# Attention scores in four quarters of the array, a shorter expert part, other warming buffer, new order

## The chip, the cores and the metric

The kernel runs on one core of a Trainium2 chip. The metric is the time of one execution on the device in microseconds; the median of several runs counts. The core's engines work side by side and wait for each other through semaphores: TensorE (PE) multiplies matrices into PSUM, VectorE (DVE), ScalarE (ACT) and GpSimd (POOL) work element by element, SyncE (SP) issues most of the DMA transfers.

## The reference

Three layers follow each other: attention in a sliding window with a bias by distance, a dense layer with an activation between two products, and a layer of eight experts that only some tokens enter.

```python
scores = scale * np.matmul(q, k.transpose(0, 1, 3, 2))          # 4 batches, 8 heads, 576 positions, 64 wide
mask = (rel >= 0) & (rel < window)                              # window = 128
scores = np.where(mask, scores + bias[None], -1000000000.0)
attn = exp(scores - max) / (sum + 1e-09);  x = attn @ v         # 2304 tokens of 512
h = x @ w_in                                                    # 512 x 2048, float64 weights
g = np.where(pos, h, np.where(neg, 0.0, (h + beta) ** 2 / (4.0 * beta)))
x = g @ w_out                                                   # 2048 x 512
do_compute = x @ w_skip > 0                                     # tokens that an expert computes
```

Tokens with a score of zero or less keep their value. With the inputs used here all 2304 scores are negative (the largest is -0.06), so no expert is entered.

## The kernel before

The 2304 tokens are nine blocks `g` of 256 (two tiles of 128), the eight heads four pairs. Class `Fused` writes attention and the dense layer as pieces of work with costs, due times and buffers; a planner in the file (`Plan.order`, line 108) gives each piece an engine and a place by the constants `PLAN`, `ENGINES`, `LAT` and `SWITCH`, and `run` (line 592) emits the pieces in that order. So the order on each engine is fixed when the program is built, and a change of the constants changes it everywhere. `SWITCH` charges TensorE for going in and out of products that use a part of the array.

`pair(g, p)` (line 305) is the attention of one block for two heads. SP loads `qkraw` (L318) and `vraw` (L321). The queries are scaled on ACT or POOL (L328, L330). The scores (L340 and L343) put the two heads into the two row halves of the array: 128 queries as weights, 256 keys (the tile and the one ahead of it) streamed, in fp32, which the trace shows as two weight loads and two products for each. They fill both buffers of the PSUM ring `att`. DVE merges the two key tiles by a mask with a predicated copy (L354), adds the bias and takes the maximum (L359); ACT computes the exponentials and their sums (L365); DVE inverts the sums (L374, L375); ACT normalizes (L393); PE transposes (L401); ACT or DVE copies to `pts` (L286 and L288 are helper lines for copies); POOL cuts the result into its two triangles `ab` (L300); PE multiplies by the values (L423), the heads side by side in the column halves of the array; ACT and DVE split the result into the two parts of `xT`.

`tile_ff` (line 492) is one step of the dense layer on one block, 256 of the 2048 middle columns: 24 products into `h` (L504, each product in three parts of a split into high and low), the activation on ACT and DVE (L516, L521, L537), the split of `g` (L286, L295), and 12 products into `acc` (L546). Eight steps make a block. Blocks 0 and 1 alternate while the weights arrive; `weight` (line 440) turns float64 into a high and a low part on POOL (L453), DVE (L457, L461, L468) and ACT.

Two more things matter. `fill` (L590) is a product without use that keeps TensorE's clock up; `run` puts such products into gaps that the planner sees before 40 us, until two buffers of the ring `acc1` are taken; they write into one buffer of that ring, which the transposes of block 0 use too. And `moe2` (line 649) counts the selected tokens (L653 to L658); every engine reads the count (L659) and branches (L660) past the code of `route` and of eight copies of `expert` if it is zero. Before, `route` is written out for 18 tiles (8 records of transposes and 16 of products each on PE), and each copy of `expert` holds 304 weight loads and products for PE in its loop (16 for transposes, 8 x 36 for the rest).

Of the kernel before, what the change touches and what calls it, by code (L numbers as in the profile page):

```python
# [11 lines left out]
F32 = mybir.dt.float32  # L12
F32R = mybir.dt.float32r
# [8 lines left out]
P = 128  # L22
# [35 lines left out]
SWITCH = {"out": 0.09, "": 0.0, "rows": 0.2, "cols": 0.14}  # L58
# [37 lines left out]
class Plan:  # L96
# [47 lines left out]
    def forward(self, free, due):  # L144
# [32 lines left out]
        while len(log) < n:  # L177
# [28 lines left out]
            if e == "T" and p.mode != mode:  # L206
                free[e] = end = end + (SWITCH["out"] if mode else 0.0) + SWITCH[p.mode]
                mode = p.mode
# [35 lines left out]
class Fused:  # L244
# [60 lines left out]
    def pair(self, g, p, due):  # L305
# [3 lines left out]
        lo = 2 * t0 - 1 if g else 0  # L309
        n = 5 if g else 4  # L310
# [8 lines left out]
            out=qk.t[:, 0:n, :].rearrange("p t j -> p (t j)"),  # L319
            in_=a["qk"][hd, :, lo:lo + n, :].rearrange("h d t j -> (h d) (t j)")), n * P * P * 4, new=[qk])  # L320
# [4 lines left out]
        def scale(e):  # L325
            q = qk.t[:, j:n:2, :]
# [19 lines left out]
        sn = self.buf("sn", 2, [P, 4, P])  # L346
        sd = add({"T": 0.87 if g else 0.66}, scores, [lq], new=s + [sn], use=[qk], mode="rows")
        st = self.buf("st", 4, [P, 2, 4])
        exps = []
        for odd, o in heads:  # L350
            h = 2 * p + odd

            def merge(e, s=s[odd]):
                nc.vector.copy_predicated(s.t[:, 1 - j:2, 0, :], self.mask[:, 1 - j:2, :], s.t[:, 1 - j:2, 1, :])  # L354

            def rowmax(e, s=s[odd], odd=odd, h=h):
                for i in range(2):
                    x = 2 * odd + i
                    nc.vector.tensor_tensor_reduce(  # L359
                        out=sn.t[:, x, :], in0=s.t[:, i, 0, :], in1=self.nrel[:, TILE_TYPE.get(t0 + i, TYPE_N), :],  # L360
# [7 lines left out]
            d = add({"D": dve(128 * (1 + j))}, merge, [sd], use=[s[odd]])  # L368
# [477 lines left out]
```

## Time and profile before

| | us |
|---|---|
| median of three runs | 535.33 (535.31 to 537.53) |
| the profiled execution | 536.52 |
| its span, first to last instruction | 534.7 |
| mean granted TensorE clock | 0.988 |

| engine | busy us | share of the span |
|---|---|---|
| PE | 516.6 | 97% |
| DVE | 280.6 | 52% |
| ACT | 293.2 | 55% |
| POOL | 108.2 | 20% |

The busy time of PE counts pipelined products whose ends are modelled, so it is read together with the chain of work that ended last. A chain row gives the start and the time until the next link; a timeline row gives the start of the first and the end of the last of several like instructions. Line numbers are those of the kernel before.

### The profile page before, as it was taken

How to read it: one execution, taken by the hardware profiler on the slowest of the kernel's cores; microseconds unless marked ns; L12 is line 12 of the kernel's file. 1: busy time of each engine (PE TensorE's matmuls, PEld its weight loads, DVE VectorE, ACT ScalarE, POOL GpSimd, SP SyncE). 2: the span in 40 equal slices, each digit the busy share in tenths (PEclk: the TensorE clock that was granted, in tenths of full speed). 3: DMA queues.
4: the chain of work that ended last, by engine and by line, in shares of the span. 5: the costliest groups of instructions: out<-in, count | busy, mean ns of one | idle time of the engine just before them, and what ended most of it. 6: DMA issues, size and time to landing. Idle time of an engine off the chain costs nothing.

```text
span 534.7 us, 9520 instructions
## 1 busy us (share of the span) xinstructions
PE 516.6 (97%) x3460; PEld 434.0 (81%) x3460; DVE 280.6 (52%) x826; ACT 293.2 (55%) x782; POOL 108.2 (20%) x208
## 2 busy tenths in 40 slices
PE   7879999999999999999999999999999999999993
PEld 3466888888888789888888898878888888789882
DVE  6899998999435523453344423541455235523231
ACT  5887565586446733663456534763376347733330
POOL 2766352344100310022002200220013000210000
PEclk9799999999999999999999999999999999999997
DMA  7665554643211121112111210120112111001001
GB/s 262 190 206 165 190 180 132 207 148 111 70 41 49 52 59 40 50 50 60 41 40 35 85 40 25 51 69 17 39 51 80 31 40 50 5 26 40 1 0 47
DMA packets 27145, 41.14 MB, mean 77 GB/s; under 512 B 2001, under 2 KB 15953, under 8 KB 27089
## 3 DMA queue, kind: packets, MB, share of 16 engines
q1 hardware_dynamic: 26416, 40.12, 23.8%
q8 instruction: 29, 0.48, 0.4%
q10 hardware_dynamic: 672, 0.33, 0.2%
q14 instruction: 28, 0.22, 0.1%
HBM read 35.72 MB, written 4.72 MB: 76 GB/s over the span
## 4 chain that ended last, share of the span: by engine, by line
PE 90%; DVE 4%; DMA 2%; issue 1%; ACT 1%; POOL 1%; ACTq 0%; POOLq 0%
PE acc L546 38%; PE h L504 37%; PE att L343 6%; PE att L423 5%; PE att L401 2%; DMA stage<-in_w_in 1%; DMA vraw<-in_v 1%; DVE sn L359 1%; DVE wtmp L468 1%; DMA qkraw<-in_qk 1%; DVE stage L461 1%; DVE att L354 0%; DVE stage L457 0%; PE acc L401 0%; ACT sn L365 0%
## 5 line engine op out<-in xcount | busy, mean ns | idle before, releaser
L504 PE MATMUL h<-xT,wi 128*128 128x256 f32 x1728 | 221.4, 282 | 0.1
L546 PE MATMUL acc<-wo,g 128*128 128x512 f32 x864 | 220.6, 400 | 0.1
L504 PEld LDWEIGHTS h<-xT,wi 128*128 128x128 f32 x1728 | 212.5, 188 | 9.1 <-issue 4.4
L546 PEld LDWEIGHTS acc<-wo,g 128*128 128x128 f32 x864 | 155.5, 188 | 40.9 <-issue 6.2
L516 ACT ACTIVATE u<-h,half 128x512 f32<-128x512 f32 x72 | 49.3, 684 | 113.0 <-PE h L504 112.8
L537 DVE SCALAR_TENSOR_TENSOR h<-h,u 128x512 f32<-128x512 f32 x72 | 50.1, 696 | 111.7 <-ACT u L521 109.4
L300 POOL TENSOR_SCALAR_AFFINE_SELECT ab<-pts 128x256 f32<-128x256 f32 (+1 forms) x144 | 62.1, 463 | 96.4 <-DVE pts L288 68.1
L365 ACT ACTIVATE sn<-sn,st 128x128 f32<-128x128 f32 x144 | 56.1, 391 | 30.7 <-DVE st L359 30.7
L286 ACT ACTIVATE g<-h 128x512 fp32r<-128x512 f32 x72 | 42.7, 593 | 34.1 <-DVE h L537 34.0
L295 DVE TENSOR_TENSOR g<-h,g 128x512 fp32r<-128x512 f32 x72 | 49.5, 687 | 18.7 <-ACT g L286 17.5
L330 POOL TENSOR_SCALAR qkraw<-qkraw,qscale 128x256 f32<-128x256 f32 x21 | 11.4, 542 | 216.7 <-DMA qkraw<-in_qk 201.5
L393 ACT ACTIVATE sn<-sn,st 128x128 f32<-128x128 f32 x144 | 46.5, 390 | 0.5 <-DVE st L375 0.3
L521 ACT ACTIVATE u<-u 128x512 f32<-128x512 f32 x72 | 45.3, 629 | 1.8
L354 DVE COPY_PREDICATED att<-mask,att 128x256 f32<-128x256 uint8 (+1 forms) x72 | 26.5, 410 | 33.4 <-PE att L343 33.3
L343 PE MATMUL att<-qkraw 64*128 64x256 f32 x272 | 40.8, 413 | 1.3 <-DVE pts L288 1.3
L453 POOL TENSOR_SCALAR wtmp<-stage 128x512 f32<-128x512 f32 x32 | 26.5, 830 | 38.8 <-DVE wi L295 14.4
L359 DVE CUSTOM_DVE_ANT_0 sn<-att,nrel 128x128 f32<-128x128 f32 x144 | 33.3, 285 | 0.0
L343 PEld LDWEIGHTS att<-qkraw 64*128 64x128 f32 x272 | 24.6, 193 | 10.6 <-issue 5.1
L423 PE MATMUL att<-ab,vraw 128*64 128x128 f32 (+1 forms) x384 | 32.0, 313 | 1.2 <-DMA vraw<-in_v 0.6
L423 PEld LDWEIGHTS att<-ab,vraw 128*64 128x64 f32 x384 | 23.1, 137 | 9.3 <-issue 2.6
L561 DVE CUSTOM_DVE_ANT_0 junk<-acc,wskip 128x512 f32<-128x512 f32 x18 | 12.4, 691 | 32.9 <-ACT stage L286 32.3
L365 ACT ACTIVATION_READ_ACCUMULATOR sn<-sn,st 128x1 f32 x144 | 27.0, 188 | 0.0
(50 smaller groups left out, 280.8 us busy)
## 6 DMA issues: line engine op xcount, KB each, us to landing
qkraw<-in_qk SPq DMA_DIRECT2D x32, 320.0 KB, 3.0
stage<-in_w_in SPq DMA_DIRECT2D x16, 512.0 KB, 3.6
stage<-in_w_out SPq DMA_DIRECT2D x16, 512.0 KB, 3.7
vraw<-in_v SPq DMA_DIRECT2D x32, 192.0 KB, 2.7
out_x<-stage SPq DMA_DIRECT2D x18, 256.0 KB, 2.0
qkraw<-in_qk SPq DMA_DIRECT2D x4, 256.0 KB, 3.4
vraw<-in_v SPq DMA_DIRECT2D x4, 128.0 KB, 4.2
nrel<-in_nrel ACTq DMA_DIRECT2D x1, 256.0 KB, 3.8
```

The costliest lines, as they stand in the source:

```text
L286: self.nc.scalar.activation(out=out, in_=in_, func=AF.Copy)
L295: eng.tensor_tensor(out=out, in0=in0, in1=in1, op=ALU.subtract)
L300: self.nc.gpsimd.affine_select(out=out, in_=in_, pattern=[[0, n], [sign, P]], compare_op=ALU.is_ge if causal else ALU.is_gt, fill=0.0, base=0,
L343: nc.tensor.matmul(s[odd].t[:, i, :, :], qk.t[o, q, :], qk.t[o, q - 1:q + 2:2, :], start=True, stop=True)
L365: nc.scalar.activation(out=sn.t[:, x, :], in_=sn.t[:, x, :], func=AF.Exp, scale=-1.0, bias=st.t[:, 0, x:x + 1], accum_out=st.t[:, 1, x:x + 1])
L393: nc.scalar.activation(out=sn.t[:, x, :], in_=sn.t[:, x, :], func=AF.Copy, scale=st.t[:, 1, x:x + 1])
L423: nc.tensor.matmul(av.t[o, out, :], v.t[:, k, o], ab.t[:, m, :], start=not more, stop=True, skip_group_check=more)
L504: nc.tensor.matmul(h.t[:, c, :], w[:, wz, k, :], x.t[:, xz, k].rearrange("p a b -> p (a b)"), start=k == 0 and i == 0, stop=k == NKC - 1 a ...
L516: r = add({"A": 0.167 + 0.213 * n}, lambda e: nc.scalar.activation(out=uv(), in_=hv(), func=AF.Relu, scale=0.5, bias=self.half), [d], new= ...
L521: nc.scalar.activation(out=uv(), in_=uv(), func=AF.Square)
L537: r = add({"D": dve(256 * n)}, lambda e: nc.vector.scalar_tensor_tensor(out=hv(), in0=hv(), scalar=1.0, in1=uv(), op0=ALU.max, op1=ALU.min ...
L546: nc.tensor.matmul(acc[i].t, gt.t[:, gz, c, i * P:(i + 1) * P], self.wo[:, f, wz, :], start=f == 0 and j == 0, stop=f == NF - 1 and j == 2)
```

## The change

- The scores take 64 queries as weights and 192 keys as stream: those that the window of a half tile can touch. Each head's two halves write to the two partition halves of its PSUM bank, so the four products of a tile (two heads, two halves) each use one quarter of the array. `qk` is laid out anew in memory for this (three key tiles and two query tiles a block); the first tile of block 0 keeps its product of 128 by 128.
- The merge becomes two predicated copies, one for each half, over 64 partitions and 64 columns a tile.
- The expert part is one function with loops over blocks, experts and quarters of the middle width. On PE its loop bodies hold 48 records (routing a block of two tiles) and 72 (one quarter of the middle width).
- The warming products write to a buffer of the ring `h`, and they go on until two other `h` buffers are taken, that is until the second dense step.
- `PLAN`, `ENGINES`, `SWITCH` and some costs change, so all pieces get a new order; the rebias of weights (L453) goes from POOL to ACT, all scaling of queries to POOL, and the normalization may go to DVE.

```diff
-PLAN = dict(base=15.36, d0=9.433, d1=4.571, d2=5, lag=1, ahead=79.42, lead=5, spread=2.882, margin=1.102, slack=0.071,
-            fin=0.107, passes=5, first=0, stick=3.899, late=0, late_due=300)
-ENGINES = dict(norm="A", wlo="DP", rebias="P", pt="AD", whi="A", square="AP", scale="AP")
+PLAN = dict(base=10.991, d0=8.647, d1=6.176, d2=5.536, lag=1, ahead=65.777, lead=10.393, spread=5.669, margin=1.2,
+            slack=0.055, fin=0.23, passes=5, first=0, stick=6, late=0, late_due=120.077)
+ENGINES = dict(norm="AD", wlo="DP", rebias="A", pt="AD", whi="A", square="AP", scale="P")
-SWITCH = {"out": 0.09, "": 0.0, "rows": 0.2, "cols": 0.14}
+SWITCH = {"": (0.0, 0.0), "rows": (0.12, 0.19), "cols": (0.135, 0.045)}
...
-            in_=a["qk"][hd, :, lo:lo + n, :].rearrange("h d t j -> (h d) (t j)")), n * P * P * 4, new=[qk])
+            in_=a["qk"][hd, :, g, 1 - j:5, :].rearrange("h d t j -> (h d) (t j)")), (4 + j) * P * P * 4, new=[qk])
...
-            q = qk.t[:, j:n:2, :]
+            q = qk.t[:, 3:5, :]
...
-        s = [self.att([P, 2, 2, P]) for _ in heads]
+        s = [self.att([P, 2, 4, 64]) for _ in heads]
 
         def scores(e):
             for i in range(2):
-                for odd, o in heads:
-                    if g == 0 and i == 0:
-                        nc.tensor.matmul(s[odd].t[:, 0, 0, :], qk.t[o, 0, :], qk.t[o, 1, :], start=True, stop=True)
-                    else:
-                        q = 2 * i + j
-                        nc.tensor.matmul(s[odd].t[:, i, :, :], qk.t[o, q, :], qk.t[o, q - 1:q + 2:2, :], start=True,
-                                         stop=True)
+                if g == 0 and i == 0:
+                    for odd, o in heads:
+                        nc.tensor.matmul(s[odd].t[:, 0, 1:3, :], qk.t[o, 3, :], qk.t[o, 1, :], start=True, stop=True)
+                    continue
+                for half in range(2):
+                    for odd, o in heads:
+                        r = slice(64 * half, 64 * half + 64)
+                        k = qk.t[o, 0:3, :].rearrange("p t (x c) -> p (t x) c", x=2)[:, 2 * i:2 * i + 4, :]
+                        k = k[:, 1:4, :] if half else k[:, 2::-1, :]
+                        nc.tensor.matmul(s[odd].t[r, i, 1 - half:4 - half, :], qk.t[o, 3 + i, r], k, start=True, stop=True)
...
-                nc.vector.copy_predicated(s.t[:, 1 - j:2, 0, :], self.mask[:, 1 - j:2, :], s.t[:, 1 - j:2, 1, :])
+                for half in range(2):
+                    r = slice(64 * half, 64 * half + 64)
+                    nc.vector.copy_predicated(s.t[r, 1 - j:2, 1 + half, :], self.mask[r, 1 - j:2, r],
+                                              s.t[r, 1 - j:2, 3 * (1 - half), :])
...
-        self.warm = self.buf("acc1", 2, [P, DM], psum=True)
+        self.warm = self.buf("h", 2, [P, 2, 256], psum=True)
...
-                    taken += b.ring == "acc1" and b is not self.warm
+                    taken += b.ring == "h" and b is not self.warm
...
-            for e in range(NE):
-                here = nc.values_load(ci[0:1, e:e + 1], min_val=0, max_val=NT)
-                with tc.If(here > 0):
-                    expert(tc, a, e, ident)
+            experts(tc, a, sel)
...
+        with tc.For_i(0, NBLK, 1) as b:
...
+        with tc.For_i(0, NE, 1) as e:
...
+            with tc.For_i(0, FE // FH, 1) as half:
...
+                with tc.For_i(0, NBLK, 1) as b:
...
+                    for f in range(FH // P):
...
+                            for i, (wz, xz) in enumerate(((0, 0), (0, 1), (1, 0))):
+                                nc.tensor.matmul(h, w1[:, wz, k, f * P:(f + 1) * P],
```

## Rows read from the trace of the kernel before

**Rows 1.** The page's busy shares, and its row of TensorE's granted clock over 40 slices.

```profile
PE 516.6 (97%) x3460; PEld 434.0 (81%) x3460; DVE 280.6 (52%) x826; ACT 293.2 (55%) x782; POOL 108.2 (20%) x208
...
PEclk9799999999999999999999999999999999999997
```

**Rows 2.** The page's chain that ended last, its shares of the span by line.

```profile
PE acc L546 38%; PE h L504 37%; PE att L343 6%; PE att L423 5%; PE att L401 2%; DMA stage<-in_w_in 1%; DMA vraw<-in_v 1%; DVE sn L359 1%; DVE wtmp L468 1%; DMA qkraw<-in_qk 1%; DVE stage L461 1%; DVE att L354 0%; DVE stage L457 0%; PE acc L401 0%; ACT sn L365 0%
```

**Rows 3.** The chain in order of time, 160 to 485 us: start, length, what.

```profile
162.67 3.02 PE h L504 x24
...
174.42 1.06 PE att L343 x8
...
184.85 1.89 PE att L423 x24
...
218.61 3.02 PE h L504 x24
...
481.26 2.82 PE h L504 x24
484.09 2.80 PE acc L546 x12
```

**Rows 4.** The timeline of PE, one pair's scores round by round: start, length, what.

```profile
174.35 0.49 PE L343 MATMUL att<-qkraw 64*128 64x256 f32 x2
...
174.67 0.38 PE L343 MATMUL att<-qkraw 64*128 64x256 f32 x2
...
174.88 0.38 PE L343 MATMUL att<-qkraw 64*128 64x256 f32 x2
...
175.41 0.50 PE L546 MATMUL acc<-wo,g 128*128 128x512 f32 x1
```

**Rows 5.** The timeline of PE, rounds of the weighted sums.

```profile
184.78 0.44 PE L423 MATMUL att<-ab,vraw 128*64 128x256 f32 x2
...
185.05 0.39 PE L423 MATMUL att<-ab,vraw 128*64 128x256 f32 x2
...
185.27 0.39 PE L423 MATMUL att<-ab,vraw 128*64 128x128 f32 x4
```

**Rows 6.** Busy us (instructions) of PE, PEld, DVE, ACT, POOL by stretch; granted clock; DMA.

```profile
20.00:30.00 10.00, 8.35 (x42) 5.21 (x43) 8.19 (x31) 8.56 (x32) 7.26 (x13) 0.67 0.50 140
50.00:120.00 70.00, 69.90 (x470) 60.92 (x470) 66.37 (x139) 43.02 (x98) 28.73 (x34) 1.00 0.51 170
```

**Rows 7.** Groups by line: xcount | busy us, mean ns of one | idle before.

```profile
L393 ACT ACTIVATE sn<-sn,st 128x128 f32<-128x128 f32 x144 | 46.5, 390 | 0.5 <-DVE st L375 0.3
...
L354 DVE COPY_PREDICATED att<-mask,att 128x256 f32<-128x256 uint8 x64 | 24.6, 426 | 30.6 <-PE att L343 30.5
...
L453 POOL TENSOR_SCALAR wtmp<-stage 128x512 f32<-128x512 f32 x32 | 26.5, 830 | 38.8 <-DVE wi L295 14.4 <-DMA stage<-in_w_in 12.5 <-DVE wo L295 9.1
...
L286 ACT ACTIVATE wi<-wtmp 128x512 fp32r<-128x512 f32 x16 | 10.1, 630 | 1.7 <-DVE wtmp L468 1.6
...
L328 ACT ACTIVATE qkraw<-qkraw,qscale 128x256 f32<-128x256 f32 x15 | 7.5, 502 | 3.2 <-DMA qkraw<-in_qk 3.2
...
L354 DVE COPY_PREDICATED att<-mask,att 128x128 f32<-128x128 uint8 x8 | 1.9, 286 | 2.8 <-PE att L343 2.8
```

**Rows 8.** The timeline of PE in the start.

```profile
8.57 2.33 PE L590 MATMUL acc<-wskip 128*128 128x512 bf16 x10
...
21.74 2.08 PE L343 MATMUL att<-qkraw 64*128 64x256 f32 x8
```

**Rows 9.** The branch after the count (L660), and the page's row of PE's code loads.

```profile
L660 ACTq EVENT_SEMAPHORE  x2: 17/17/17, 532.6 to 532.7; - x2
...
L660 ACTq COMPARE_BRANCH  x1: 54/54/54, 528.9 to 528.9; - x1
...
L660 PEldq COMPARE_BRANCH  x1: 4238/4238/4238, 529.0 to 529.0; - x1
...
q8 instruction: 29, 0.48, 0.4%
```

More of the change, by code (lines that the diff above doesn't have):

```diff
@@ L206, in forward @@
             if e == "T" and p.mode != mode:
-                free[e] = end = end + (SWITCH["out"] if mode else 0.0) + SWITCH[p.mode]
+                free[e] = end = end + SWITCH[mode][1] + SWITCH[p.mode][0]
                 mode = p.mode
@@ L424, in avs @@
                                      skip_group_check=more)
-        d = add({"T": 0.93 if g else 0.71}, avs, [lv, last[0][2], last[1][2]], new=[av], use=[v, last[0][1], last[1][1]],
+        d = add({"T": 0.92 if g else 0.71}, avs, [lv, last[0][2], last[1][2]], new=[av], use=[v, last[0][1], last[1][1]],
                 mode="cols")
@@ L582, in constants @@
         nc.vector.memset(ones, 1.0)
-        nc.gpsimd.affine_select(out=ones, in_=ones, pattern=[[0, 2], [-1, P]], compare_op=ALU.is_ge, fill=0.0,
-                                base=0, channel_multiplier=1)
+        nc.gpsimd.affine_select(out=ones, in_=ones, pattern=[[0, 2], [1, P]], compare_op=ALU.is_gt, fill=0.0,
+                                base=0, channel_multiplier=-1)
         nc.vector.tensor_copy(self.mask, ones)
@@ L589, in fill @@
         w = self.wskip.bitcast(BF16)
-        self.nc.tensor.matmul(self.warm.t, w[:, 0:P], w[:, 0:DM], start=True, stop=True)
+        self.nc.tensor.matmul(self.warm.t.rearrange("p a b -> p (a b)"), w[:, 0:P], w[:, 0:DM], start=True, stop=True)
     def run(self):
@@ L645 @@
 FE = 1024
-NFE = FE // P
+FH = 256
 def moe2(tc, a, sk, sel, one, toti):
@@ L660, in moe2 @@
         with tc.If(total > 0):
-            ident = c.tile([P, P], F32, tag="ident", name="ident")
-            nc.sync.dma_start(out=ident, in_=a["ident"])
-            ci = c.tile([1, NE], I32, tag="ci", name="ci")
-            with ExitStack() as ctx:
-                route(ctx, tc, a, sel, one, ident, ci)
-            for e in range(NE):
-                here = nc.values_load(ci[0:1, e:e + 1], min_val=0, max_val=NT)
-                with tc.If(here > 0):
-                    expert(tc, a, e, ident)
@@ new lines, in experts @@
+def experts(tc, a, sel):
+    nc, out = tc.nc, a["out"]
+    with ExitStack() as ctx:
+        c = ctx.enter_context(tc.tile_pool(name="mc", bufs=1))
+        p2 = ctx.enter_context(tc.tile_pool(name="mp2", bufs=2))
+        ps = ctx.enter_context(tc.tile_pool(name="mps", bufs=2, space=PSUM))
+        ident = c.tile([P, P], F32, tag="ident", name="ident")
+        nc.sync.dma_start(out=ident, in_=a["ident"])
+        wg = c.tile([P, NKC, NE], F32, tag="wg", name="wg")
+        nc.sync.dma_start(out=wg, in_=a["w_gate"].rearrange("(k p) e -> p k e", p=P))
+        iota = c.tile([P, NTILE, NE], F32, tag="iota", name="iota")
+        for e in range(NE):
+            nc.vector.memset(iota[:, :, e], float(e))
+        lg = c.tile([P, NTILE, NE], F32, tag="lg", name="lg")
+        xr = c.tile([P, NBLK, 2, NKC, 256], F32R, tag="xr", name="xr")
@@ L790, in expert @@
-            nc.scalar.dma_start(out=out[bass.ds(b * 256, 256), :].rearrange("(t p) n -> p t n", p=P), in_=x)
+                nc.scalar.activation(out=xt[:, :, t * P:(t + 1) * P], in_=xp, func=AF.Copy)
+                for k in range(NKC):
+                    nc.tensor.matmul(lp[:, t, :], xt[:, k, t * P:(t + 1) * P], wg[:, k, :], start=k == 0,
+                                     stop=k == NKC - 1)
+            nc.vector.tensor_copy(lg[:, bass.ds(b * 2, 2), :], lp)
+            part = lambda z: xr[:, bass.ds(b, 1), z].rearrange("p o k n -> p (o k) n")
@@ new lines, in experts @@
+            nc.scalar.activation(out=part(0), in_=xt, func=AF.Copy)
+            nc.vector.tensor_tensor(out=part(1), in0=xt, in1=part(0).bitcast(F32), op=ALU.subtract)
+        bc = lambda ap: ap.unsqueeze(2).to_broadcast([P, NTILE, NE])
+        mx = c.tile([P, NTILE], F32, tag="mx", name="mx")
+        col = c.tile([P, NTILE], F32, tag="col", name="col")
+        w = c.tile([P, NTILE, NE], F32, tag="w", name="w")
+        hot = c.tile([P, NTILE, NE], F32, tag="hot", name="hot")
+        nc.vector.tensor_reduce(out=mx, in_=lg, op=ALU.max, axis=AX.X)
@@ new lines, in experts @@
+        nc.vector.tensor_reduce(out=col, in_=w, op=ALU.add, axis=AX.X)
+        nc.vector.tensor_scalar_add(col, col, 1e-9)
+        nc.vector.reciprocal(col, col)
+        gate = c.tile([P, NTILE, NE], F32, tag="gate", name="gate")
+        nc.vector.tensor_tensor(out=gate, in0=hot, in1=bc(col), op=ALU.mult)
+        add = c.tile([P, NTILE, DM], F32, tag="add", name="add")
+        nc.vector.memset(add, 0.0)
+        w1 = c.tile([P, 2, NKC, FH], F32R, tag="w1", name="w1")
+        w2 = c.tile([P, 2, FH // P, DM], F32R, tag="w2", name="w2")
@@ L793, in build @@
+        x = c.tile([P, NTILE, DM], F32, tag="x", name="x")
+        rows = out.rearrange("(t p) n -> p t n", p=P)
+        nc.sync.dma_start(out=x, in_=rows)
+        nc.vector.tensor_tensor(out=x, in0=x, in1=add, op=ALU.add)
+        nc.sync.dma_start(out=rows, in_=x)
 def build(tc, a):
```

165 lines of the change are left out of this document (55 added, 110 removed).

## Prediction

> **What bounds the kernel now.** I read the page's busy shares first: TensorE (PE) is busy 97% of the span, VectorE (DVE) 52%, ScalarE (ACT) 55%, GpSimd (POOL) 20% [rows 1]. A busy PE need not be the bound, so the chain that ended last comes second: three quarters of it are the two products of the dense layer (L504, L546), and the attention's scores (L343), weighted sums (L423) and transposes (L401) are nearly all of the rest [rows 2]. Third, the chain in order of time. The same pattern comes back with a period of 218.61 - 162.67 = 55.94 us, one block of 256 tokens. In the last block, which has no attention beside it, a step of the dense layer is 2.82 + 2.80 = 5.62 us, so eight steps are 45.0 us [rows 3]. The other 10.9 us of a period are the four attention pairs of the next block, 2.73 us a pair, of which the scores are the dearest visit: 1.06 us from their first product to the next dense product, and then 0.20 us more, since the first dense group after a visit takes 3.02 instead of 2.82 [rows 3]. From 50 us on PE has no idle time (69.90 of 70 us) although DVE is at 66.4 of 70 there [rows 6]; so in seven of nine blocks (g = 2 to 8, 28 pairs) a nanosecond taken off PE is a nanosecond off the span, and work on the other engines is covered.
>
> Outside of this lie two places. Nine blocks of 45.0 and 36 pairs of 2.73 make 503 us, but the last dense products end at about 526 us: some 23 us are lost, all before 55 us, where attention of g = 0 and 1 runs as chains through ACT and DVE. And after the last product come 8.4 us, in which each engine reads one number and branches past the expert code (with these inputs no token is selected, so none of it runs): PE's branch takes 4238 ns, and ACT's next instruction after a branch at 528.9 starts at 532.6 [rows 9].
>
> **Scores by quarters.** A pair's scores before are eight product records, two for each fp32 matmul, in four rounds: the two heads sit in the two row halves of the array and start together. The first three rounds start at 174.35, 174.67 and 174.88, and the next dense product, after the fourth, at 175.41 [rows 4]; so the first takes 0.32 (0.215 of streaming, the rest the load of 128 weight columns that nothing hides), two take 0.215, the last 0.31 with the emptying of the array: 1.06. The change halves the queries of a product to 64 and cuts the keys from 256 to 192. That makes sixteen records with four quarters at once, still four rounds, each 192/256 x 0.215 = 0.161 us: 4 x 0.054 = 0.215 less. The first load has 64 columns; the weighted sums, whose weights have 64 columns, show a first round of 0.27 where the scores show 0.32 [rows 4, 5]: 0.05 less. Three quarters start behind the first, some 0.02 more. That is 0.24 us a pair, with 0.20 and 0.27 as ends; 28 pairs give **-6.7 us** (-5.6 to -7.5). The pairs of g = 0 and 1 lie in the stretch that PE doesn't bound, and in g = 0 half of the products stay 128 wide: nothing counted.
>
> That all four quarters run at once no row shows. Row halves run together in the scores, column halves in the weighted sums [rows 4, 5], and four streams of 64 partitions read as many bytes as the two of 128 partitions there. I take the full overlap; the ends are in the rivals. What also counts against it is the rate of issue: sixteen products in 0.65 us is one in 40 ns, and the fastest stream shown, four products with 128 columns in the same 0.39 us that two with 256 take [rows 5], is four in a round of 0.215, one in 54 ns. But there the columns themselves set the pace, 128 being half of 256, and within a round two products start so close that the rows give them one time; I therefore take no limit from issue.
> The Trainium skill's page "TensorE: Matmul & The Clock Gate" (Part 2: What happens when you issue a matmul) says that the sequencer needs about 62 ns a matmul where its decoding is done in microcode; sixteen would then be 0.99 us, and the scores would gain nothing. The 54 ns of [rows 5] lie below that already, so the trace speaks against the rule here.
>
> **The merge on DVE.** One predicated copy of 128x256 a head (426 ns) becomes two of 64 partitions and 128 elements; the nearest row, 128x128, has 286 ns [rows 7]. That is 0.15 more a head, 0.3 a pair at most. In the 28 pairs it hides behind PE (DVE is far from full after 120 us); for g = 2, in the stretch with 66.4 of 70, it is 1.2 us that only hold as long as PE has other work. In the start it is up to 8 x 0.2 = 1.6 us of a nearly full DVE.
>
> **Engines and order.** L453 (32 x 830 ns) leaves POOL for ACT, where no row shows it; ACT's copies of the same 128x512 take 630 ns, so about 20 us, 12 pieces of it before 55 us. Fifteen scalings (502 ns) leave ACT for POOL, eight of them before 55 us, and some of the normalizations (390 ns each, four a pair) may go to DVE [rows 7]. In the start ACT thus gets about 7.5 us and loses 4 plus whatever normalizations move; POOL, freed of 9 us there, can take low halves of weights from DVE. After 120 us all of this is covered by PE. POOL works in order: a scaling that waits for its `qk` load holds up the causal masks (L300) queued behind it, and the weighted sums wait for these; after 120 us the distance of a block covers it, in the start nothing does. SP's queue issues the loads of `qk`, `v` and weights in the new order, and a late one shows up in the same place. I put the whole at nothing, with 3 us either way, since in the start ACT and DVE are both near full and one's relief is the other's load. The new due times place pairs anew in a period: visits can't be fewer than four for the scores (a pair takes both `att` buffers) and two joined ones for the sums, and that is what the chain shows already (24 records in 1.89 us [rows 3]); so order can lose there, not gain.
>
> **Warming products.** They stop before at 10.9 us (the last ten at 8.57 [rows 8]), as two `acc1` buffers are then taken. PE then has gaps, and the granted clock of 20 to 30 us is 0.67 of full, the mean of its levels 2.4 and 1.2 GHz; eight scores take 2.08 us in it [rows 6, 8], twice the 1.06 of later. With the `h` ring they go on until the second dense step, some 20 us longer, so the gaps are filled. Worth: 0 if the DVE chain is late anyway, up to 3 us (0.33 x 10 / 0.5 = 6.6 us at half clock, halved). I take 1.5, less 0.5 for the longer merges: **-1.0 us** for the start, with -4 to +4 as ends together with the engines.
>
> **Expert part.** None of it runs; only its length counts. Before, PE alone skips 18 x 24 + 8 x 304 = 2864 records; after, 48 + 72 = 120 plus loop control. PE's code came in 29 fetches [rows 9] for its 6920 loads and products [rows 1], some 239 a fetch: before, the target lies a dozen fetches ahead, after within one. So I take the wait for the branch away: 532.6 - 528.9 less the 0.3 that a read and step cost: **-3.4 us** (0 to -3.8). The final barriers wait for the slowest engine, so one engine that still has to fetch, DVE with its many short operations first, gives all of it back.
> The Trainium skill's page "Runtime: NRT & Kernel Launch" (Instruction fetch mechanics) has it that only a taken branch to a target outside of the two pages held forces a fetch; by that the term is the full one. No row shows a branch that stays inside.
>
> **Sum.** The profiled execution took 536.52 us with a span of 534.7. -6.7 - 1.0 - 3.4 = -11.1: span 523.6, run 525.4. The median of the runs (535.33) lies 1.19 under the profiled one, so the forecast is **524.2 us**.
>
> **Rivals.** (1) The expert part is shorter but the branch still waits, on one engine at least: 524.2 + 3.4 = 527.6. For it: no row shows a short branch; against it: the count of records. 0.25. (2) Issue bounds the sixteen products: at 54 ns they take 0.86, as long as before; scores gain nothing, 530.9. 0.06. (3) The order loses: weighted sums are no longer joined, two visits more a block at some 0.4 (0.1 in the first round, 0.1 in the last, 0.20 after it, as for the scores), 7 x 0.8 = 5.6, or the start gets 4 us worse: about 529. 0.09. (4) Slower: the quarters of one row half don't overlap, so eight rounds of 0.161 take the place of four of 0.215: +0.43 less the 0.05 of the load, 0.38 x 28 = +10.6 and some 1.5 in the start: 535.3 + 12.1 - 4.4 = 543. It turns slower as soon as rounds exceed six. For it: no row with four at once; against it: both halves overlap by themselves. 0.05.
>
> **How the numbers follow.** Forecast 0.55, rivals 0.45. The range leaves out (4) and the far ends: down to 519.5 (all terms at their good ends: -7.5, -4, -3.8, some of which exclude each other), up to 531, which takes in (1) to (3). A measurement of this kernel can tell about 0.5%, 2.7 us: faster means under 532.6. Forecast and (1) to (3) hold 0.95; of these 0.05 fall within the bound and 0.02 beyond it, where one of them meets a start at its bad end. So faster 0.88, same 0.05, slower 0.07 with (4).
>
> **What would show it.** The period of a block after 160 us falls from 55.94 to about 55.0; the scores' rows show sixteen records in about 0.80 us with rounds 0.16 apart, four at one time. The granted clock of 20 to 30 us is near 1.0, and L590 goes on past 20 us. PE's branch (now at L660) is far under 4 us and the last instruction lies under 5 us behind the last read. Wrong it would be with a period unchanged (rival 2), longer (4), more separate visits of L423 (3), or a branch of 4 us (1).

## The result, and the profile after

| | before | after |
|---|---|---|
| median of the runs, us | 535.32 | 528.97 |
| the profiled execution, us | 536.52 | 528.84 |
| its span, us | 534.7 | 527.1 |
| end of the last dense product, us | 526.3 | 521.8 |
| mean granted clock | 0.988 | 0.998 |

The changed kernel takes 0.9873 of the time of before, with a 95% interval of 0.9847 to 0.9899: 6.35 us less, where 11.1 were forecast. The time lies in the range, 4.8 us over the forecast itself.

First the page after: the busy shares, the granted clock, the chain that ended last by engine, and the merges.

```profile
PE 514.0 (98%) x3760; PEld 430.2 (82%) x3760; DVE 303.0 (57%) x912; ACT 281.4 (53%) x738; POOL 103.6 (20%) x206
...
PEclk9999999999999999999999999999999999999999
...
PE 82%; DVE 11%; ACT 2%; issue 1%; DMA 1%; POOL 1%; ACTq 0%; POOLq 0%; SPq 0%; DVEq 0%
...
L357 DVE COPY_PREDICATED att<-mask,att 64x128 f32<-64x128 uint8 (+1 forms) x144 | 41.5, 288 | 9.5 <-PE att L345 5.1
```

Against [rows 1], PE is as busy as ever and DVE 22 us busier. DVE's part of the chain has grown to 11%; the page before has this row:

```profile
PE 90%; DVE 4%; DMA 2%; issue 1%; ACT 1%; POOL 1%; ACTq 0%; POOLq 0%
```

The merges are now 144 copies of 64 partitions, 41.5 us of busy time in place of 26.5.

The chain in order of time, one period and the last dense products (start, length, what):

```profile
245.81 3.03 PE h L508 x24
...
270.95 0.81 PE att L345 x16
271.76 1.61 PE h L508 x12
...
288.84 1.89 PE att L427 x24
...
300.79 3.03 PE h L508 x24
...
513.39 8.42 PE acc L550 x36
```

The period is 300.79 - 245.81 = 54.98 us where [rows 3] have 55.94: the 0.96 forecast. A visit of the scores takes 0.81 instead of 1.06 with the same 1.61 - 1.41 = 0.20 behind it. Its rounds, from the timeline of PE:

```profile
270.88 0.39 PE L345 MATMUL att<-qkraw 64*64 64x192 f32 x4
...
271.42 0.34 PE L345 MATMUL att<-qkraw 64*64 64x192 f32 x4
...
271.69 0.39 PE L508 MATMUL h<-xT,wi 128*128 128x256 f32 x1
```

Four products start within 0.02 us in the first round (270.88), the last four start at 271.42, and the next dense product at 271.69. The three rounds before the last take 0.54 together, so one streams for about 0.16, as worked out from [rows 4] by 192/256, and the first carries 0.05 more for the load of its weights.

The tail is short now. After the branch (line 664 after):

```profile
L664 PEldq COMPARE_BRANCH  x1: 358/358/358, 524.6 to 524.6; - x1
...
L664 DVEq EVENT_SEMAPHORE  x1: 21/21/21, 525.2 to 525.2; - x1
```

PE's branch takes 358 ns in place of the 4238 of [rows 9], and DVE goes on at 525.2. From the end of the last dense product to the end of the span it is 5.3 us instead of 8.4.

So two of the three terms came as forecast. Where the rest went, a table of three stretches shows, each from the trace: to the end of block 2's last dense product, from there to the last dense product, and the tail.

| us | to the end of block 2 | six blocks after it | tail | span |
|---|---|---|---|---|
| before | 206.3 | 320.0 | 8.4 | 534.7 |
| after | 207.8 | 314.0 | 5.3 | 527.1 |
| difference | +1.5 | -6.0 | -3.1 | -7.6 |

The six blocks gain 0.25 a pair in their 20 pairs, 5.0; the other 0.9 is a wait for a load of `v`, issued at 354.6 us, that the profiled execution of before has and the changed one has not. The first stretch was to bring -1.0 from the start and -1.9 from the eight pairs of g = 2 and 3; it is 1.5 us longer in these two executions. The chain of the changed kernel, first between 28 and 30 us, then a piece from 58 to 62 us, shows why to look at DVE:

```profile
28.14 0.30 DVE att L357
...
28.46 0.31 DVE att L357
...
28.80 0.30 DVE att L357
...
29.12 0.31 DVE att L357
...
29.46 0.29 DVE sn L363
...
58.52 0.42 DVE stage L461
58.94 0.64 DVE h L541
59.58 0.59 DVE stage L465
60.17 0.60 DVE wtmp L472
60.77 0.60 DVE g L295
61.37 0.60 DVE wtmp L472
```

The four merges of a pair start 0.33 apart and take 1.29 us together, each with 0.02 or 0.03 us of gap behind it. The two of the kernel before, from its timeline of DVE, took 0.74:

```profile
38.10 0.74 DVE L354 COPY_PREDICATED att<-mask,att 128x256 f32<-128x256 uint8 x2
```

With 0.415 each, two of them one behind the other would be 0.83: the second starts before the first has ended, which the copies of the changed kernel never do. And from 53 to 99 us the chain is nearly all DVE, as in the second piece: weights (L461, L465, L472, L295), dense layer (L541), merges. A window from 60 to 120 us has DVE full (third pair of numbers, of 60 us), first before, then after:

```profile
60.00:120.00 60.00, 59.90 (x390) 52.42 (x389) 57.13 (x124) 38.19 (x89) 24.07 (x28) 1.00 0.51 170
...
60.00:120.00 60.00, 58.59 (x407) 51.49 (x406) 59.24 (x129) 47.02 (x96) 3.72 (x6) 1.00 0.55 182
```

### The profile page after: what moved, and what is told of

The parts are those of the page before. It is cut to its first block, busy times and chain, and to the rows that moved or that the text cites. A ratio compares the mean times of both kernels' runs of the same rounds, so it can differ in the third digit from the quotient of the medians.

```text
span 527.1 us, 10132 instructions
## 1 busy us (share of the span) xinstructions
PE 514.0 (98%) x3760; PEld 430.2 (82%) x3760; DVE 303.0 (57%) x912; ACT 281.4 (53%) x738; POOL 103.6 (20%) x206
## 4 chain that ended last, share of the span: by engine, by line
PE 82%; DVE 11%; ACT 2%; issue 1%; DMA 1%; POOL 1%; ACTq 0%; POOLq 0%; SPq 0%; DVEq 0%
PE acc L550 35%; PE h L508 34%; PE att L427 5%; PE att L345 5%; PE att L405 2%; DVE att L357 2%; DVE stage L465 2%; DVE wtmp L472 1%; DMA qkraw<-in_qk 1%; DVE stage L461 1%; DVE sn L363 1%; DVE h L541 1%; POOL ab L300 1%; ACT sn L369 1%; DVE wi L295 1%
## 5 line engine op out<-in xcount | busy, mean ns | idle before, releaser
L508 PE MATMUL h<-xT,wi 128*128 128x256 f32 x1728 | 225.0, 282 | 1.4 <-DVE g L295 1.4
L550 PE MATMUL acc<-wo,g 128*128 128x512 f32 x864 | 216.4, 397 | 0.0
L369 ACT ACTIVATE sn<-sn,st 128x128 f32<-128x128 f32 x144 | 56.2, 392 | 65.1 <-DVE st L363 65.1
L541 DVE SCALAR_TENSOR_TENSOR h<-h,u 128x512 f32<-128x512 f32 x72 | 50.3, 698 | 70.3 <-ACT u L525 69.0
L300 POOL TENSOR_SCALAR_AFFINE_SELECT ab<-pts 128x256 f32<-128x256 f32 (+1 forms) x144 | 61.5, 462 | 86.5 <-ACT pts L286 65.1
L295 DVE TENSOR_TENSOR g<-h,g 128x512 fp32r<-128x512 f32 x72 | 49.7, 690 | 32.7 <-ACT g L286 32.4
L527 POOL TENSOR_TENSOR u<-u 128x512 f32<-128x512 f32 x19 | 19.9, 1046 | 198.6 <-ACT u L520 198.6
L357 DVE COPY_PREDICATED att<-mask,att 64x128 f32<-64x128 uint8 (+1 forms) x144 | 41.5, 288 | 9.5 <-PE att L345 5.1
L363 DVE CUSTOM_DVE_ANT_0 sn<-att,nrel 128x128 f32<-128x128 f32 x144 | 33.5, 286 | 1.1
L525 ACT ACTIVATE u<-u 128x512 f32<-128x512 f32 x53 | 33.3, 629 | 1.2
L328 POOL TENSOR_SCALAR qkraw<-qkraw,qscale 128x256 f32<-128x256 f32 x36 | 19.6, 544 | 71.4 <-DMA qkraw<-in_qk 69.6
L345 PE MATMUL att<-qkraw 64*64 64x192 f32 x544 | 31.4, 342 | 0.3 <-issue 0.3
L378 DVE TENSOR_SCALAR st<-st 128x4 f32<-128x4 f32 x36 | 9.8, 273 | 36.6 <-ACT sn L369 36.6
L397 ACT ACTIVATE sn<-sn,st 128x128 f32<-128x128 f32 x80 | 27.4, 396 | 4.8 <-DVE st L379 4.5
```

The lines of the kernel that those rows point to most:

```text
L295: eng.tensor_tensor(out=out, in0=in0, in1=in1, op=ALU.subtract)
L300: self.nc.gpsimd.affine_select(out=out, in_=in_, pattern=[[0, n], [sign, P]], compare_op=ALU.is_ge if causal else ALU.is_gt, fill=0.0, base=0,
L345: nc.tensor.matmul(s[odd].t[r, i, 1 - half:4 - half, :], qk.t[o, 3 + i, r], k, start=True, stop=True)
L357: nc.vector.copy_predicated(s.t[r, 1 - j:2, 1 + half, :], self.mask[r, 1 - j:2, r], s.t[r, 1 - j:2, 3 * (1 - half), :])
L363: nc.vector.tensor_tensor_reduce(out=sn.t[:, x, :], in0=s.t[:, i, 1:3, :].rearrange("p x c -> p (x c)"), in1=self.nrel[:, TILE_TYPE.get(t0 ...
L369: nc.scalar.activation(out=sn.t[:, x, :], in_=sn.t[:, x, :], func=AF.Exp, scale=-1.0, bias=st.t[:, 0, x:x + 1], accum_out=st.t[:, 1, x:x + 1])
```

## Experiments

Theory A: the quarters gain what was forecast, and the new order and engine lists lost the rest in the start. Theory B (sharpened to C after the first four runs): up to 120 us DVE is a bound as much as PE, and the longer merges give back there what the quarters gain after it. Ratios are against runs of the kernel before on the same chip; there its runs reach from 534.7 to 541.0, and its first stretch alone, in kernels with the same order and operations, from 206.3 to 209.5. So I read the three stretches beside the times.

A part of this scatter can be seen in the products of `fill`. The ten at 8.57 us in [rows 8] take 2.33 us; the same ten, in the kernel with the short expert part alone, take

```profile
9.51 4.26 PE L590 MATMUL acc<-wskip 128*128 128x512 bf16 x10
```

0.43 us each instead of 0.22, so at 1.2 instead of 2.4 GHz. The records of the granted clock begin, at its full level, at 6.2 us in the first execution and at 13.4 in the second. A row ahead of these records shows 1.00 all the same, and the mean clock of the first table leaves this part out. In the changed kernel they begin at 13.2 us.

**The quarters alone.** Layout, scores, mask and merges of the changed kernel in the kernel before; costs and constants, so the order on every engine, as before.

```diff
 # kernel before
-        s = [self.att([P, 2, 2, P]) for _ in heads]
+        s = [self.att([P, 2, 4, 64]) for _ in heads]      # and scores(), merge(), layout of the change
         sd = add({"T": 0.87 if g else 0.66}, scores, ...   # costs unchanged
```

> The kernel before with the quarter scores, their layout and the two merges alone; costs and constants of the order are those of before, so every engine's order is that of before. Theory A (the new order and engines lost what is missing): the 28 pairs that PE bounds give 0.24 us each, -6.7, and the longer merges cost at most 1 in the start: 528 to 530 us. Theory B (the merges themselves, on a DVE that is full up to 120 us, took the gain of the early blocks): only the 20 pairs of g = 4 to 8 show, -5.0, and the early part gets some 2 us later: 532 to 533 us.

Measured: 545.83 us, ratio 1.015 (1.011 to 1.0189). Slower than either theory had it. The first stretch ends at 215.5, nine microseconds late, and the period is 56.2, longer than before although a visit of the scores takes 0.81 to 0.88. The chain inside a period (start, length, what) shows what took the gain:

```profile
241.23 0.29 DVE sn L363
...
241.89 0.41 PE att L405 x2
...
244.31 1.27 ACT sn L397 x4
245.58 0.58 ACT u L520
...
246.18 0.64 ACT u L525
...
246.87 0.30 DVE att L357
...
248.18 0.41 PE att L405 x2
```

PE's transposes (L405) come where the old order has them, but the maximum (L363) behind the longer merges now ends later, and they wait for it: PE stands still for 0.43 us in front of 241.89 and again in front of 248.18. The gain is spent on waits. In an order that is fixed, 0.55 us more a pair on DVE isn't hidden even in the late blocks.

**The quarters with costs that fit them.** As above, but the planner is told of 0.7 for the scores and 0.64 for a head's merges; constants and engine lists as before.

```diff
-        sd = add({"T": 0.87 if g else 0.66}, scores, ...
+        sd = add({"T": 0.7 if g else 0.55}, scores, ...
-            d = add({"D": dve(128 * (1 + j))}, merge, ...
+            d = add({"D": 2 * (0.32 if g else 0.24)}, merge, ...
```

> The kernel before with the quarter scores and with planner costs that fit them (scores 0.7, merges 0.64 a head); constants and engine lists of before, so the order is made anew. If q_only was slow because its order counted on the short merge, the period comes down to about 55.0 and the time to 533 to 536 us. If the old engine lists can't carry the longer merges in the start whatever the order, the period is 55.0 but the end of block 2 stays 8 to 10 us late: 538 to 541 us.

Measured: 539.61 us, ratio 1.0064 (1.0032 to 1.0096). The period is 54.9: with an order that knows of the merges the late blocks gain in full. The end of block 2 stays late, at 214.9. So the second half of the expectation holds.

**The expert part alone.**

```diff
-                    expert(tc, a, e, ident)
+            experts(tc, a, sel)
```

> The kernel before with the short expert part alone. Both theories: the branch no longer waits, about 3.1 us less (535.3 to 532.2), all of it behind the last dense product; the profile's end of the last dense product stays at about 526.

Measured: 534.64 us, ratio 0.9927 (0.9888 to 0.9965); the tail is 5.3 us against 8.4, PE's branch 356 ns (row of line 660):

```profile
L660 PEldq COMPARE_BRANCH  x1: 356/356/356, 531.6 to 531.6; - x1
```

The term is the expected one. The last dense product ends at 528.8 and not at about 526: block 2 is done at 209.5, in an execution whose clock came to its full level at 13.4 us.

**The warming products alone.**

```diff
-        self.warm = self.buf("acc1", 2, [P, DM], psum=True)
+        self.warm = self.buf("h", 2, [P, 2, 256], psum=True)
...
-                    taken += b.ring == "acc1" and b is not self.warm
+                    taken += b.ring == "h" and b is not self.warm
```

> The kernel before with the warming products in the ring h alone. If the half clock between 20 and 27 us lay on the chain, 1 to 3 us less (532.5 to 534.3); if DVE and ACT set the start, no change within 0.5 us. The granted clock of 20 to 30 us should be 1.0 either way.

Measured: 535.56 us, ratio 0.9965 (0.9945 to 0.9985). The granted clock between 20 and 30 us is 1.00 instead of the 0.67 of [rows 6] (columns as there):

```profile
20.00:30.00 10.00, 9.80 (x59) 5.12 (x58) 9.50 (x39) 8.25 (x32) 6.79 (x13) 1.00 0.55 155
```

The clock was restored; by the ratio that is 1.9 us, with 0.8 and 3.0 as the ends of its interval. The trace can't tell where: the profiled execution is the slowest of ten (537.84), and in it block 2 ends at 207.9.

**The new order alone.** Constants, engine lists and planner costs of the change in the kernel before.

```diff
-PLAN = dict(base=15.36, d0=9.433, d1=4.571, d2=5, ...
+PLAN = dict(base=10.991, d0=8.647, d1=6.176, d2=5.536, ...
-ENGINES = dict(norm="A", wlo="DP", rebias="P", pt="AD", whi="A", square="AP", scale="AP")
+ENGINES = dict(norm="AD", wlo="DP", rebias="A", pt="AD", whi="A", square="AP", scale="P")
```

> The kernel before with the new constants of the order, the new engine lists and the new costs alone; scores, merges, warming and expert part as before. Theory A: the new engine lists put 13 us of normalizations and most low halves of weights on DVE and leave POOL idle, which costs 3 to 5 us up to 120 us: 538 to 540 us. Theory B: the order by itself costs nothing, 534 to 536 us, or gains.

Measured: 532.24 us, ratio 0.9899 (0.986 to 0.9937). Theory A is refuted: the order is a gain. Block 2 ends at 203.0, 3.3 us before that of the kernel before, with the scores of before. The granted clock of 20 to 30 us is 1.00 here too, with the old warming (columns as in [rows 6]):

```profile
20.00:30.00 10.00, 7.21 (x55) 5.09 (x55) 9.56 (x37) 9.82 (x37) 8.36 (x15) 1.00 0.67 201
```

**The changed kernel with the scores of before.** The order of the changed kernel, wide scores, one merge a head.

```diff
 # kernel after
+        full = True
...
 # in scores()
+                if full:
+                    for odd, o in heads:
+                        nc.tensor.matmul(whole(s[odd])[:, i], qk.t[o, 3 + i, :], qk.t[o, i:i + 2, :], start=True, stop=True)
+                    continue
 # in merge()
+                if full:
+                    w = whole(s)
+                    nc.vector.copy_predicated(w[:, 1 - j:2, 1, :], self.mask[:, 1 - j:2, :], w[:, 1 - j:2, 0, :])
+                    return
```

> The changed kernel with the scores of before (128 queries by 256 keys, one merge a head) in the order of the changed kernel; all costs of the planner, the warming and the expert part stay as changed. Theory C (up to 120 us DVE is the bound, and the longer merges give back there what the quarters win later): the period after 160 us goes back to about 55.9, 5 us longer in all, and the part up to the end of block 2 gets 3 to 5 us shorter: 528 to 530 us, no difference from the changed kernel. Theory D (the quarters win 7 us and the new order loses in the start): 534 to 536 us.

Measured: 530.37 us, ratio 0.988 (0.9828 to 0.9932). Block 2 ends at 202.9, 4.9 before that of the changed kernel; the period is 55.86. The two nearly cancel, as theory C has it. DVE's merges up to 120 us, here in 22 copies (L363) and in the changed kernel in 44 (L357), differ by 4.2 us of busy time, and the gaps between the copies come on top (changed kernel first):

```profile
0.00:120.00 120.00, 11.65 (x44) 1.00 0.57 186
...
0.00:120.00 120.00, 7.43 (x22) 1.00 0.60 194
```

All other operations come in the same order on every engine in both kernels, so the two traces can be laid beside each other. That shows where the 4.9 us are lost, and it is for the most part ahead of the stretch that the chain puts on DVE. The changed kernel's first dense product is already 3.4 us late (changed kernel first, then wide scores):

```profile
31.46 3.08 PE L508 MATMUL h<-xT,wi 128*128 128x256 f32 x24
...
28.05 3.08 PE L518 MATMUL h<-xT,wi 128*128 128x256 f32 x24
```

At 53 us it is 4.5 late, at 74 us 3.6, at 99 us 5.3. Up to 20 us, in the attention of g = 0, 3.0 of it come about. The merges of a pair there take 1.02 instead of 0.49, which is 2.1 us for four pairs (changed kernel, wide scores; the first load of `qk` came 0.4 sooner in the former):

```profile
6.26 1.02 DVE L357 COPY_PREDICATED att<-mask,att 64x64 f32<-64x64 uint8 x4 [2.84 <-PE att L345]
...
6.67 0.49 DVE L363 COPY_PREDICATED att<-mask,att 128x128 f32<-128x128 uint8 x2 [3.26 <-PE att L344]
```

And the eleven products of `fill` in front of the transposes take 1.4 us longer on the chain, since the clock comes to its full level at 13.2 us in the one and at 10.1 in the other (changed kernel, wide scores):

```profile
10.00 4.07 PE h L594 x11
...
9.76 2.66 PE h L604 x11
```

Whether the longer merges delay the clock, or whether it falls out differently from one execution to the next, as in the kernel before, no run here shows.

A part of the difference to the changed kernel isn't the scores': the tail is 7.1 instead of 5.3, and the rows of its branch (line 674) show that DVE alone waited, from 524.4 to 527.7:

```profile
L674 DVEq COMPARE_BRANCH  x1: 72/72/72, 524.4 to 524.4; - x1
...
L674 DVEq EVENT_SEMAPHORE  x1: 21/21/21, 527.7 to 527.7; - x1
```

This is what rival (1) says, met in a neighbour of the changed kernel: with the short code, too, one engine can still wait. Without these 1.8 us the kernel with wide scores would stand at 528.6, beside 528.97.

**Fewer merges in the early blocks.** The changed kernel without the second merge of each head in g = 1 and 2: the keys that it would bring into those scores are left out.

```diff
-                for half in range(2):
+                for half in range(1 if 0 < g < 3 else 2):
                     r = slice(64 * half, 64 * half + 64)
                     nc.vector.copy_predicated(s.t[r, 1 - j:2, 1 + half, :], self.mask[r, 1 - j:2, r],
```

> The changed kernel with the second of the two merges of each head left out in the pairs of g = 1 and 2 (their result is not the reference's), everything else and the order the same: 16 copies of some 0.33 us less, 5.3 us of DVE before 120 us. Theory C: the end of block 2 comes 3 to 5 us sooner, 524 to 526 us. Theory D (the early part waits for ACT, POOL or the loads): less than 1 us, 528 to 529 us.

Measured: 524.3 us, ratio 0.9754 (0.9698 to 0.981); block 2 ends at 203.5, 4.3 us sooner, though PE's and all other work is the same and the clock comes to its full level no sooner (13.8 us). That shows DVE's time in g = 1 and 2 as the bound, and the merges as the cost. It also shows what one copy costs. The two copies of a pair that are left both start at partition 0, and they overlap:

```profile
28.08 0.48 DVE L357 COPY_PREDICATED att<-mask,att 64x128 f32<-64x128 uint8 x2
```

Each takes 0.28 us, and they start 0.20 apart. The same copies start 0.33 apart in the changed kernel, where partitions 0 and 64 take turns. So a pair's merges shrink from 1.29 to 0.48, by more than the two copies that are gone.

**Wide scores early, quarters late.** The edit of the kernel with the scores of before, with

```diff
+        full = g < 3
```

> The changed kernel with the scores of before in the blocks g = 0 to 2, whose merges fall in the stretch with a full DVE, and quarters in g = 3 to 8, in the order of the changed kernel. Theory C: the early part of the kernel with full scores and the period of 54.97 of the changed one: 524 to 526 us, faster than both. Theory D: as the changed kernel or slower by the scores' 0.25 us in eight pairs: 529 to 531 us.

Measured: 522.95 us, ratio 0.9737 (0.9685 to 0.9788), against 0.9873 of the changed kernel: the best kernel of this study, 6.0 us under the changed one. Block 2 ends at 202.3, the period is 54.9. In the window of 60 to 120 us DVE is as full as in the changed kernel, but PE now has no gap (60.00 instead of 58.59):

```profile
60.00:120.00 60.00, 60.00 (x383) 53.03 (x382) 59.26 (x135) 47.60 (x104) 4.62 (x7) 1.00 0.55 188
```

**The old engine lists in the changed kernel.**

```diff
-ENGINES = dict(norm="AD", wlo="DP", rebias="A", pt="AD", whi="A", square="AP", scale="P")
+ENGINES = dict(norm="A", wlo="DP", rebias="P", pt="AD", whi="A", square="AP", scale="AP")
```

> The changed kernel with the engine lists of before (normalization on ACT alone, rebias on POOL, scaling on ACT or POOL), ordered anew by the changed constants. If taking work from POOL and giving DVE normalizations is what fills DVE, the early part gets shorter by some of the 13 us of normalizations: 525 to 528 us. If the new lists are the better ones, 531 to 534 us.

Measured: 539.73 us, ratio 1.0046 (1.0021 to 1.0072), 11 us above the changed kernel (9 by the ratios), outside of both expectations; block 2 ends at 219.2.

**Only the rebias back on POOL.**

```diff
-... rebias="A", ...
+... rebias="P", ...
```

> The changed kernel with the rebias of weights back on POOL as the only change of the engine lists, ordered anew. If POOL's work beside DVE is what makes DVE's operations on the weights longer (785 and 723 ns before, 686 and 683 after, in 60 to 120 us), most of the 10 us between the old and the new lists come back with it: 535 to 539 us, with L465 and L472 above 700 ns. If ACT's normalizations were the matter, 529 to 531 us.

Measured: 540.73 us, ratio 1.0091 (1.0058 to 1.0124); block 2 ends at 218.5. DVE's L465 between 60 and 120 us, first in this kernel, then in the changed one (count | busy us, mean ns):

```profile
L465 DVE SCALAR_TENSOR_TENSOR stage<-stage 128x512 int32<-128x512 int32 x16 | 11.9, 751 | 0.1
```

```profile
L465 DVE SCALAR_TENSOR_TENSOR stage<-stage 128x512 int32<-128x512 int32 x19 | 13.0, 686 | 0.1
```

The operations on the weights are longer when POOL works beside DVE, as expected, and the order isn't the reason, for one trace alone shows it. Of the 64 operations L465 and L472 in this kernel, the 25 with POOL idle beside them take 660 to 707 ns; the 23 that run beside POOL's rebias range from 660 to 1140, with 850 as their mean. All 64 together take 4.9 us more than in the changed kernel. That is less than half of the 10.7 us by which block 2 ends later; for the rest the order was made anew, and the next two runs show how much that alone can do.

**New orders with better costs.** The changed kernel with 0.64 as the cost of a head's merges; and the kernel with wide early scores with costs of 0.95, 0.38 and 0.64.

```diff
 # the first of the two
-            d = add({"D": 2 * dve(64 * (1 + j)) + 0.06}, merge, ...
+            d = add({"D": 2 * (0.32 if g else 0.24)}, merge, ...
```

> The changed kernel with the planner's cost of a head's merges set to 0.64 (0.48 in g = 0) instead of 0.47, ordered anew; the operations are the same. DVE's work before 120 us doesn't shrink by it. If DVE is the bound there, 527.5 to 530 us; if only the order's error about the merges cost the early part, 524 to 526 us.

> The scores of before in g = 0 to 2 and quarters in g = 3 to 8, as hybrid_g3, but with planner costs of 0.95 for the wide scores, 0.38 for their merges and 0.64 for the quarters' merges, ordered anew. If costs nearer to the rows let the planner place the early pairs better, 521 to 523 us; if hybrid_g3's order was good as it is, 522 to 525 us.

Measured: 535.87 us, ratio 0.9968 (0.9936 to 0.9999), with block 2 at 217.2; and 530.95 us, ratio 0.9902 (0.9868 to 0.9936), with block 2 at 210.3. Both expectations fail: the same operations in another order of the same planner, with costs nearer to the rows, lose 7 and 8 us (5 and 9 by the ratios), all of it before the end of block 2, while the period of both is 54.8. A part is lost with the clock. PE has gaps in these orders, and the granted clock falls to half in stretches, which in the changed kernel it doesn't between 13.2 us and the tail. In the first of the two kernels PE is busy for 8.07 of the 10 us from 50 to 60, and the clock is 0.52 in

```profile
55.00:62.00 7.00, 6.66 (x27) 4.52 (x28) 6.48 (x22) 5.01 (x15) 3.92 (x5) 0.52 0.62 178
```

In the second the clock is 0.87 from 40 to 50 us, and in the kernel with the old engine lists 0.83 from 40 to 60 us. How much of the loss is the clock's and how much the waits' isn't separated.

## Why the prediction was right, and where it wasn't

**The sum.** Direction and range held; the forecast missed by 4.8 us. It was carried by three terms, and one of them, the largest, gives nothing in the sum. In its place the order, put at nothing, brought 4 to 5 us. So the number is right in part by luck. Rival (3) names about 529 too, but for an order that loses, and this one gains. The low end of the range is 0.5 lower than its terms give: 535.3 - 7.5 - 4 - 3.8 = 520.0, not 519.5.

**The quarters.** The working from [rows 4] and [rows 5] was right in every number: four quarters at once, rounds of 0.16, 0.05 off the first load, 0.25 a pair measured for 0.24 forecast. Rivals (2) and (4) fall with these rows. The Trainium skill's page "TensorE: Matmul & The Clock Gate" (Part 2: What happens when you issue a matmul), with some 62 ns a matmul where microcode decodes, isn't what this case shows: sixteen products start within 0.56 us.

The step that failed is the price of the merges: at most 1.6 us in the start, of which the sum took 0.5, and nothing behind 50 us, where they were to hide behind PE. The prediction said that from 50 us on a nanosecond off PE is one off the span, since PE has no idle time in 69.90 of 70 us, and that DVE at 66.4 of 70 would hold [rows 6]. Both readings were of the state before. The runs show 4.9 us lost up to the end of block 2 against wide scores in the same order, 3.4 of it at the first dense product, with a clock that rose later in that execution; and 4.3 us come back when the second copies of g = 1 and 2 alone are left out, with the same late clock. The price was low for a reason: 0.15 more a head came from the 286 ns of [rows 7], the length of one copy, without asking how one follows the other. Two wide copies overlap, four half ones don't, and a pair costs 0.53 more in g = 0 (1.02 - 0.49) and 0.55 later (1.29 - 0.74), not 0.2 and 0.3. The rule that speaks against this change stands in the Trainium skill's page "VectorE: DVE Perf Modes" (Two Vector instructions with no wait between them), and the prediction missed it: an instruction whose operands start in another group of 32 partitions than those in front of it starts only when these have finished. The copies start at partitions 0 and 64 in turn, and the trace agrees: gaps of 0.02 to 0.03 us between them, where the wide copies, all from partition 0, overlap by 0.09, and so do half copies that all start there, in the kernel with fewer merges. An order that does the same halves of both heads one behind the other was not run with all copies. The gain of the late blocks and the loss of the early ones (4.6 and 4.9 between the changed kernel and the same with wide scores) cancel. So the quarters as built bring about nothing; used from g = 3 on they bring 6.

**Order and engines.** These were put at nothing, with 3 us either way, on the ground that the visits of PE can't be fewer and that ACT and DVE are both near full. The new order alone brought 3.3 us to the end of block 2, 4.4 in the span and 0.0101 x 535 = 5.4 in the ratio, part of which is the scatter of the kernel before. This is most of what the change gains beside the tail. The sentence that order can lose there and not gain looked at the late blocks alone; the room was in the start. Why this order is the better one stays open: POOL beside DVE makes DVE's operations longer (850 against 683 ns on the mean in one trace), and the lists that take work from POOL go with the better times, but orders with other costs and the same lists scatter by as much. No run here changes an engine without a new order. The prediction also named the risk that a scaling on POOL waits for its load of `qk` and holds up the masks (L300). The chain of the changed kernel has this from 42.7 to 51.8 us, but the kernel with wide scores has the same scaling and masks on its chain, 4 us sooner.

**Warming products.** The mechanism came (clock 1.00 where it was 0.67). In the kernel before it is worth 1.9 us by the ratio (0.8 to 3.0), which takes in the 1.5. In the changed kernel it is worth nothing that shows: the new order has 1.00 between 20 and 30 us with the old warming too, and ends block 2 at 203.0, the kernel with wide scores and the new warming at 202.9. The term was worked out on the gaps of the old order.

**The tail.** -3.1 for -3.4. The rule of the Trainium skill's page "Runtime: NRT & Kernel Launch" (Instruction fetch mechanics), that only a target outside of the pages held makes a taken branch wait, agrees with PE's 358 ns here. DVE's 3.3 us in the kernel with wide scores show that the short code alone doesn't decide it. What made DVE wait there stays open: loads of code follow the branch by 1 us in that trace, as they do in the changed kernel, whose DVE goes on at once.

**The calibration.** The profiled execution of before lay 1.19 us above its median, and I took this offset over to the changed kernel. Its profiled execution lies on its median, so the offset didn't carry over: the change is 7.7 us by the profiled executions and 6.35 by the medians, and 1.2 of the 4.8 us of the miss are this offset. Of the 7.7, the wait of 0.9 us for `v` belongs to that execution of before and to no term.

## What to carry to other kernels

A full engine that isn't on the chain is the next bound: before work is put on it, ask how much more it can take in that very stretch, not what the share over the span is. Price an operation by the distance to the next start, not by its length alone. Where two kernels have the same order, lay their traces beside each other product by product: the chain tells what the time is spent on, the lag tells where it is lost. A change that trades PE's time for DVE's is worth most where DVE is idle, and it can be made for these blocks alone. And in a kernel whose order is fixed in advance, a longer step needs a new order before it is judged, while a new order by itself moves the time by as much as the step.

## What the runs showed of the hardware

Products on four quarters of the array (64 rows by 64 columns each) ran at full overlap in fp32: sixteen in four rounds of 0.16 us; the four of a round start within 0.02 us. Two predicated copies from partition 0 overlapped by 0.09 us (0.415 each, 0.74 together); half copies from partition 0 overlapped too (0.28 each, 0.20 apart); those that start at partitions 0 and 64 in turn didn't overlap at all (0.30 each, 0.33 apart). DVE's operations on 128x512 int32 took 660 to 707 ns with POOL idle and up to 1140 beside POOL's rebias, in one trace. The clock came to its full level at 6.2 us in one execution and at 13.4 in another of kernels that differ in the expert part alone; until then products of 512 bf16 columns started 0.43 us apart, behind it 0.22. A taken branch cost PE 0.36 us over short code and 4.24 over long, and DVE was left waiting for 3.3 us in one of the kernels with short code.
